# Attention and top-1 MoE: all shifts of a pair first on VectorE, one rotating PSUM pool of four banks, the selection steps at new slots

## The chip, the cores and the metric

The kernel runs on one core of one Trainium2 chip. The metric is the device time of one execution in microseconds. The engines are TensorE (PE; its weight loads are PEld), VectorE (DVE), ScalarE (ACT), GpSimd (POOL) and SyncE (SP), which issues most transfers. Each engine takes its instructions in the order in which they were written for it, and waits where one's input or buffer isn't ready.

## The reference

Causal attention over 8 batches of 12 heads (448 positions, 64 wide) feeds a mixture of 8 experts in which each token goes to one expert and each expert takes at most 80 tokens, those with the largest gate weight.

```python
scores = scale * np.matmul(q, k.transpose(0, 1, 3, 2))
scores = np.where(mask, -1000000000.0, scores)
scores = scores - np.max(scores, axis=-1, keepdims=True)
attn = np.exp(scores)
attn = attn / (np.sum(attn, axis=-1, keepdims=True) + 1e-09)
x = np.matmul(attn, v)                  # heads side by side: 3584 tokens x 768
logits = x @ w_gate                     # 8 experts
expert_idx = np.argmax(logits, axis=1)
gate_w = softmax(logits)[arange, expert_idx]
for e in range(8):
    tok_idx = the 80 tokens of expert e with the largest gate_w
    out[tok_idx] = gate_w[tok_idx, None] * (np.maximum(x[tok_idx] @ w1[e], 0) @ w2[e])
```

Tokens that no expert takes give rows of zeros.

## The kernel before

**The pairs.** Heads go two by two, 6 pairs to a batch, 48 in all. `pairs` is one list, and the loop over it takes three pairs at once in a software pipeline: at step i the scores of pair i are normalized, the probabilities of pair i-1 are transposed, and pair i-2 is multiplied with the values. A step has 8 slots (`SLOTS`), and the order of the code in a slot is the order on the engines. Two pairs are a third (`PH`): GpSimd splits the next third's q and k in two f16 parts (`split_third`, L370 and L402) while this one runs.

**One step.** TensorE first multiplies pair i-2's probabilities with v (`xp`, eight products), then the scores of the pair's first block (three `corner` products to `sp`). In slots 1, 2, 4 and 5 (`TSLOT`) it transposes four groups of four blocks of pair i-1 (`tp`). In the last slot it makes the 18 score products of pair i+1 (`sp`), in four banks.

VectorE "shifts" each of the seven score tiles of pair i: one instruction adds the mask, negates, and leaves the row's minimum in `nb` (L446, to `ns`). ScalarE raises it to a power with `nb` as its bias (L449, `prob`). Tiles come in the order (0,0), (0,1), (1,0), (1,1), (2,0), (2,1), first; they are 192, 192, 320, 320, 448, 448 and 64 wide, and slot k holds the shift and the power of tile k. ScalarE also copies each group of transposes to `PT` (L486) in slots 2 to 5; of the fourth group two small pieces are copied by VectorE. VectorE copies `xp` to `xu` (L509) in slot 2 (`XSLOT`).

**The selection.** After a batch's six pairs come its gate and its selection, in steps spread over the slots of the next pairs. `STEPS` names the slot, counted from the batch's end, and `later_on` files the step under it: `gp`/`gs` gate products and their copy, `lp`/`lg`/`logit` logits by token and their largest, `chosen` to `parts` the one-hot and the weight in three parts, `r0t` to `r1c` their transposes (`selt`) and copies (`ex`), `rl`/`lt`/`cp`/`ro` the comparison with the tokens kept so far, `c3w` to `c0l` the comparison of the batch's tokens with each other (`rn`, `less`), `gt`/`own`/`earlier`/`rank` the ranks, `places` (`rm`), `rr`, `tn`, `tab`, `rp` and `row` the new table of kept tokens. `ROWS0` and `ROWS1` place eight row groups: TensorE transposes `xu` back (`rt`), VectorE scales (`xr`), and SyncE writes the token rows (`xs`). `norms` inverts the sums (L533) and copies a part of them to `rql` on ScalarE.

**PSUM.** There are eight banks: four for scores (`ps_s`), two for transposes (`ps_t`), two for all the rest (`ps_m`: `xp` and every tile of the selection and the row groups, through `bank`). A request waits until the tile that had the bank last has been read.

**After the pairs.** `TAIL` is the written order of the last batch's rest, and after it come the experts: two layers each, with weights loaded by SyncE and split by ScalarE and VectorE.

Of the kernel before, what the change touches and what calls it, by code (L numbers as in the profile page):

```python
# [7 lines left out]
F32 = mybir.dt.float32  # L8
# [4 lines left out]
AF = mybir.ActivationFunctionType  # L13
ALU = mybir.AluOpType
# [3 lines left out]
P = 128  # L18
DH = 64
QB = 64  # L20
MASKED = -8.0e9
HUGE = 3.0e38
TSLOT = [1, 2, 4, 5]
CSLOT = [2, 3, 4, 5]
XSLOT = 2
NORMS = [0, 2, 2]
ROWGAP = 1
ROWS0 = [3, 6, 9, 11]
ROWS1 = [20, 22, 25, 45]
STEPS = {'gp': 13, 'gs': 14, 'lp': 18, 'lg': 18, 'logit': 19, 'shifted': 20, 'chosen': 21, 'sums': 22, 'one_hot': 23, 'weight': 23, 'columns': 24, 'weighted': 25, 'parts': 26, 'r0t': 29, 'r0c': 30, 'r1t': 31, 'r1c': 32, 'rl': 33, 'lt': 34, 'c3w': 35, 'c3l': 36, 'cp': 37, 'ro': 38, 'c2w': 38, 'c2l': 39, 'c1w': 40, 'c1l': 40, 'c0w': 41, 'c0l': 41, 'places': 42, 'gt': 44, 'own': 44, 'earlier': 44, 'rank': 45, 'rr': 47, 'tn': 50, 'tab': 50, 'rp': 53, 'row': 54}  # L30
THIRD = [0, 0, 2, 2, 4, 6, 8]
THIRD_EARLY = [0, 2, 4, 6, 6, 8, 9]
SECOND = [5, 6, 7, 8, 9, 10, 11]
# [13 lines left out]
def attention_then_moe(  # L47
# [30 lines left out]
    wearly = ctx.enter_context(tc.tile_pool(name="wearly", bufs=1))  # L78
    sel_stack = ExitStack()
    spool = sel_stack.enter_context(tc.tile_pool(name="sel", bufs=2, side="right"))  # L80
    ps_m = ctx.enter_context(tc.tile_pool(name="ps_m", bufs=2, space=PSUM))
    att = ExitStack()
    akeep = att.enter_context(tc.tile_pool(name="akeep", bufs=1))
    apool = att.enter_context(tc.tile_pool(name="att", bufs=2))
    turn_stack = ExitStack()
    ps_t = turn_stack.enter_context(tc.tile_pool(name="ps_t", bufs=2, space=PSUM))
    score_stack = ExitStack()
    ps_s = score_stack.enter_context(tc.tile_pool(name="ps_s", bufs=4, space=PSUM, side="right"))
    ps_x = None

    def bank(shape, dtype, name):
        return (ps_x or ps_m).tile(shape, dtype, name=name, tag="x" if ps_x else "misc")

    row_banks, row_pool = [], []

# [312 lines left out]
    def scores_groups(pr, n):  # L408

        st = state[pr.b * HB + pr.p // PH]  # L410
        p = pr.p % PH
        pr.P = prob[n % 2]
        pr.sp = {}

        def products():
            q_hi, q_lo, k_hi, k_lo = st["parts"]
            banks = [ps_s.tile([P, 512], F32, name="sp", tag="sp") for _ in range(4)]
            for j in range(2):
                pr.sp[0, j] = banks[j][:, 0:WIDTH[0]]
                pr.sp[1, j] = banks[j][:, WIDTH[0]:WIDTH[0] + WIDTH[1]]  # L420
                pr.sp[2, j] = banks[2 + j][:, 0:WIDTH[2]]
            pr.sp["first"] = banks[2][:, WIDTH[2]:WIDTH[2] + QB]
            for t in range(NT - 1):
                for x, (a, c) in enumerate(((q_hi, k_hi), (q_lo, k_hi), (q_hi, k_lo))):
                    for j, rows in enumerate((lo, hi)):
                        nc.tensor.matmul(pr.sp[t, j], a[rows, p, queries(t)], c[rows, p, FROM[t]:FROM[t] + WIDTH[t]], start=(x == 0),  # L426
                                         stop=(x == 2))
# [7 lines left out]
        def after(t, j):
            h = t * H + 2 * pr.p + j
            return lambda: softmax(pr.sp[t, j], WIDTH[t], mask[:, MASK_AT[t]:MASK_AT[t] + WIDTH[t]], OFF[t, j], pr.sums[:, h:h + 1])

        def after_first():
            h = (NT - 1) * H + pr.p  # L440
            softmax(pr.sp["first"], QB, mask_0, OFF["first"], pr.sums[:, h:h + 1])

        def softmax(sp, w, m, off, total):
            ns = apool.tile([P, S], F32, name="ns", tag="ns", bufs=4)
            nb = apool.tile([P, 1], F32, name="nb", tag="nb", bufs=5)
            pr.masked = nc.vector.tensor_tensor_reduce(  # L446
                out=ns[:, 0:w], in0=sp, in1=m, scale=-1.0 / 8.0, scalar=HUGE, op0=ALU.add, op1=ALU.min,
                accum_out=nb)
            nc.scalar.activation(pr.P[:, off:off + w], ns[:, 0:w], AF.Exp, bias=nb, scale=-1.0, accum_out=total)  # L449

        return products, products_first, [after(t, j) for t in range(NT - 1) for j in range(2)] + [after_first]

    def transpose_groups(pr, n):

        pr.PT = flipped[n % 2]

        full = lambda t, j, at: pr.P[:, OFF[t, j] + at * QB:OFF[t, j] + at * QB + P]
        blocks = [
            [full(t, j, t) for j in range(2) for t in (0, 1)],
            [full(t, j, 2 * t + 1) for j in range(2) for t in (1, 2)],  # L460
            [full(2, j, at) for j in range(2) for at in (3, 1)],
            [full(0, j, 2) for j in range(2)] + [full(2, j, -1) for j in range(2)],
        ]
        ways = [
            [(slice(0, P), 0, [[256, 2], [1, 256]], COL[0] + QB, [[WPT, 2], [1, 256]])],
            [(slice(0, P), 0, [[256, 2], [1, 256]], COL[1] + QB, [[WPT, 2], [1, 256]])],
            [(slice(0, P), 0, [[256, 2], [P, 2], [1, P]], COL[0] + S - P,
              [[WPT, 2], [COL[3] - P - (COL[0] + S - P), 2], [1, P]])],
            [(hi, QB, [[256, 2], [P, 2], [1, QB]], COL[2], [[COL[3] - COL[2], 2], [WPT, 2], [1, QB]]),
             (lo, QB, [[P, 2], [1, QB]], COL[1], [[WPT, 2], [1, QB]]),  # L470
             (lo, 256, [[QB, 2], [1, QB]], COL[0], [[WPT, 2], [1, QB]])],
        ]

        def group(g):
            got = []

            def work():
                tp = ps_t.tile([P, 4 * P], F32, name="tp", tag="tp")
                got.append(tp)
                for i, f in enumerate(blocks[g]):  # L480
                    nc.tensor.transpose(tp[:, i * P:(i + 1) * P], f, ident)  # L481

            def copy(x):
                rows, at, dims, to, todims = ways[g][x]
                way = nc.scalar.copy if x == 0 else nc.vector.tensor_copy
                way(part_of(pr.PT, rows, to, *todims), part_of(got[0], rows, at, *dims))  # L486
            return work, [lambda x=x: copy(x) for x in range(len(ways[g]))]
        return [group(g) for g in range(4)]

    def values_group(pr):  # L490
# [94 lines left out]
    def row_group(bt, t, g, how="v"):  # L585
# [5 lines left out]
        def turn():  # L591
            if ps_x:

                own = len(row_banks) % 2
                tp = (ps_t if own else ps_m).tile([P, NH, P], F32, name="rt", tag="tp" if own else "misc",
                                                  padded_shape=[P, 4, P])
# [98 lines left out]
    def select_groups(bt):  # L695
# [61 lines left out]
        def table_chunk(s):  # L757
# [15 lines left out]
                bt.lower.append((lower, sn))  # L773

            def counts():
                cp = got["cp"] = (ps_m.tile([SL, E], F32, name="cp", tag="misc") if last else bank([SL, E], F32, "cp"))
# [29 lines left out]
        def later_part(t):  # L806

            if t == NT - 1:
                bt.gt = ps_m.tile([P, NT, E], F32, name="gt", tag="misc")
# [133 lines left out]
    def batch_plan(bt):  # L943

        ends = (bt.b * NP + NP) * SLOTS
        for x, f in zip(NORMS, norms(bt, slice(0, NP))):
            later_on(ends + x, [f])
        for g, at in enumerate((ROWS0, ROWS1)):
            for t in range(NT):
                later_on(ends + at[t], row_group(bt, t, g), ROWGAP)  # L950

        steps = dict(zip(("gp", "gs"), gate_products(bt, range(NH))))
        steps.update(gate_steps(bt))
        if CAP:
            steps.update(select_groups(bt))
        for name, at in STEPS.items():
            if name in steps:
                later_on(ends + at, [steps.pop(name)])
        assert not steps
# [5 lines left out]
    with tc.manual_schedule():  # L965
# [26 lines left out]
        for i, pr in enumerate(pairs):  # L992
# [25 lines left out]
            for k in range(SLOTS):  # L1018
# [15 lines left out]
                if k == SLOTS - 1 and i + 1 < n:
# [386 lines left out]
```

## Time and profile before

| what | us |
|---|---|
| median of 3 runs | 598.86 (598.81 to 599.22) |
| the profiled execution | 603.67 |
| its span, from the first to the last instruction | 601.6 |
| busy in the span: PE, DVE, ACT, POOL | 472.4, 389.8, 405.0, 238.2 |
| first and last copy of xp to xu | 25.3 and 464.4 |

The profiled execution is 4.8 us above the median, and 2.07 us of it lie outside the span. The pairs end with the copy at 464.4; the rest of the last batch and the experts fill what is left of the span. In a row of the timeline the first number is the start in us from the span's start, the second the duration in us; what stands in brackets is how long the engine was idle before it, and what ended that. In a row of waits the numbers are the sum in us, the count and the longest. In a row of the chain of work that ended last, the two numbers are start and length.

### The profile page before, as it was taken

To read this page: it belongs to the slowest core of one execution; us is meant where nothing else is said; L and a number is where in the kernel's file an instruction comes from. 1 tells how busy PE (TensorE), PEld (TensorE's weight loads), DVE (VectorE), ACT (ScalarE), POOL (GpSimd) and SP (SyncE) were. 2 spreads that over 40 slices of the span, in tenths; PEclk is the share of its full clock that TensorE was granted. 3 is DMA by queue.
4 is the path that set the end of the run, shared out by engine and by line. 5 is a ranking of instruction groups with operands and counts; after the bars stand their busy time and mean duration, and the time that the engine had idled before them with its cause. 6 is when DMAs were issued, how large, how long until landed. Compare 5 with 4: busy or idle time off the path is not lost. (4 is left out here: it accounts for less than half of the span.)

```text
span 601.6 us, 15237 instructions
## 1 busy us (share of the span) xinstructions
PE 472.4 (79%) x5530; PEld 335.3 (56%) x5530; DVE 389.8 (65%) x1305; ACT 405.0 (67%) x1081; POOL 238.2 (40%) x345
## 2 busy tenths in 40 slices
PE   2878877887677777778777687788678899899995
PEld 1544454554354545545454454455445589899985
DVE  4554576556675565565655755656563789999993
ACT  3776766766666657565756665576654869998982
POOL 6636342526252543335243526142301442664321
PEclk9998999899999999897989998979897999999999
DMA  6333544456054515352525362343386379999971
GB/s 211 124 128 109 164 129 153 160 183 208 25 185 159 183 24 199 134 171 61 195 101 172 95 217 91 125 139 117 115 347 204 120 259 383 388 385 404 406 299 34
DMA packets 46666, 109.90 MB, mean 183 GB/s; under 512 B 5842, under 2 KB 23250, under 8 KB 45952
## 3 DMA queue, kind: packets, MB, share of 16 engines
q1 hardware_dynamic: 45392, 105.20, 50.0%
q0 software_dynamic: 1056, 3.51, 1.8%
q8 instruction: 43, 0.70, 0.5%
q14 instruction: 31, 0.25, 0.1%
q10 hardware_dynamic: 144, 0.23, 0.1%
HBM read 85.35 MB, written 23.99 MB: 182 GB/s over the span
## 5 line engine op out<-in xcount | busy, mean ns | idle before, releaser
L449 ACT ACTIVATE prob<-ns,nb 128x192 f32<-128x192 f32 (+3 forms) x336 | 177.4, 529 | 111.9 <-DVE nb L446 103.9
L481 PE MATMUL tp<-ident,prob 128*128 128x128 f32 x768 | 123.4, 291 | 59.9 <-ACT PT L486 59.6
L446 DVE CUSTOM_DVE_ANT_0 ns<-sp,mask 128x192 f32<-128x192 f32 (+3 forms) x336 | 138.2, 440 | 6.7 <-PE sp L426 3.8
L486 ACT COPY PT<-tp 128x512 f32<-128x512 f32 x192 | 100.2, 522 | 49.0 <-PE tp L481 47.3
L481 PEld LDWEIGHTS tp<-ident,prob 128*128 128x128 f32 x768 | 86.9, 146 | 81.0 <-ACT PT L486 77.5
L426 PE MATMUL sp<-qk 64*128 64x448 f16 (+2 forms) x864 | 85.8, 313 | 47.7 <-DVE nb L446 40.7
L504 PE MATMUL xp<-PT,vt 128*64 128x448 f32 (+3 forms) x768 | 104.7, 419 | 1.7 <-DVE PT L486 1.1
L370 POOL TENSOR_TENSOR qk<-qk,qk 128x448 f16<-128x448 f32 x93 | 97.1, 1061 | 14.5 <-DVE qk L402 8.7
L1150 DVE SCALAR_TENSOR_TENSOR wl<-wraw,wh 128x768 f16<-128x768 f32 (+1 forms) x98 | 97.3, 1059 | 1.9 <-POOL wl L1341 1.6
L504 PEld LDWEIGHTS xp<-PT,vt 128*64 128x64 f32 x768 | 55.2, 148 | 63.2 <-issue 30.6
L1165 ACT ACTIVATE wh<-wraw 128x768 f16<-128x768 f32 (+1 forms) x98 | 84.9, 927 | 3.8 <-ACT yt L1292 0.9
L426 PEld LDWEIGHTS <-qk 64*128 64x128 f16 x864 | 38.3, 98 | 84.3 <-issue 66.4
L486 DVE COPY PT<-tp 64x128 f32<-64x128 f32 x96 | 23.1, 278 | 91.6 <-ACT PT L486 91.6
L1226 PEld LDWEIGHTS <-wh 128*128 128x128 f16 x668 | 67.1, 100 | 3.8 <-issue 3.8
L1228 PEld LDWEIGHTS <-wh 128*128 128x128 f16 x668 | 66.7, 100 | 2.0 <-issue 1.9
L1229 PEld LDWEIGHTS <-wl 128*128 128x128 f16 x668 | 66.7, 100 | 0.9 <-issue 0.9
L509 DVE COPY xu<-xp 128x448 f32<-128x448 f32 x48 | 29.9, 624 | 55.8 <-PE xp L504 55.8
L449 ACT ACTIVATION_READ_ACCUMULATOR prob<-ns,nb 128x1 f32 x336 | 63.3, 188 | 0.0
L402 POOL CAST qk<-qk 128x896 f16<-128x896 f32 x40 | 36.5, 931 | 51.3 <-PE sp L426 43.5
L1307 POOL DMA_INDIRECT out<-yo,idx x8 | 34.7, 4341 | 54.8 <-ACT yo L1304 51.6
L1228 PE MATMUL op<-hl,wh 128*128 128x80 f16 x324 | 36.9, 202 | 1.3 <-issue 1.3
L1229 PE MATMUL op<-hh,wl 128*128 128x80 f16 x324 | 36.9, 202 | 1.2 <-issue 1.2
(175 smaller groups left out, 669.6 us busy)
## 6 DMA issues: line engine op xcount, KB each, us to landing
wraw<-w SPq DMA_DIRECT2D x48, 384.0 KB, 9.5
wraw<-w SPq DMA_DIRECT2D x30, 512.0 KB, 9.8
out<-mask SPq DMA_DIRECT2D x56, 192.0 KB, 2.5
qk<-k_t SPq DMA_DIRECT2D x23, 448.0 KB, 4.0
qk<-q_t SPq DMA_DIRECT2D x23, 448.0 KB, 4.1
vt<-v_t SPq DMA_DIRECT2D x24, 384.0 KB, 7.8
xs<-xr SPq DMA_DIRECT2D x42, 192.0 KB, 1.8
wraw<-w SPq DMA_DIRECT2D x5, 1536.0 KB, 7.8
```

The lines of the kernel that those rows point to most:

```text
L370: sub = lambda e, o, a, b: e.tensor_tensor(out=o, in0=a, in1=b, op=ALU.subtract)
L426: nc.tensor.matmul(pr.sp[t, j], a[rows, p, queries(t)], c[rows, p, FROM[t]:FROM[t] + WIDTH[t]], start=(x == 0), stop=(x == 2))
L446: pr.masked = nc.vector.tensor_tensor_reduce(out=ns[:, 0:w], in0=sp, in1=m, scale=-1.0 / 8.0, scalar=HUGE, op0=ALU.add, op1=ALU.min, accum ...
L449: nc.scalar.activation(pr.P[:, off:off + w], ns[:, 0:w], AF.Exp, bias=nb, scale=-1.0, accum_out=total)
L481: nc.tensor.transpose(tp[:, i * P:(i + 1) * P], f, ident)
L486: way(part_of(pr.PT, rows, to, *todims), part_of(got[0], rows, at, *dims))
L504: nc.tensor.matmul(xp[rows, c * P:S], st["vt"][:, c, p * P + j * DH:p * P + (j + 1) * DH], pr.PT[:, j, n0:n0 + w], start=(c == 0), stop=(c ...
L1150: return nc.vector.scalar_tensor_tensor(out=l, in0=src, scalar=SW, in1=h, op0=ALU.mult, op1=ALU.subtract)
L1165: nc.scalar.activation(h, src, AF.Copy, scale=SW)
L1226: nc.tensor.matmul(o, wh[:, ws], ah[:, c, :], start=(x == 0 and i % per == 0), stop=False, skip_group_check=True)
L1228: nc.tensor.matmul(o, wh[:, ws], al[:, c, :], start=False, stop=False, skip_group_check=True)
L1229: nc.tensor.matmul(o, wl[:, ws], ah[:, c, :], start=False, stop=(x == n - 1), skip_group_check=True)
```

## The change

1. **Shifts first.** `softmax` returns the shift and the power apart. `SHIFTED` puts the shifts of a pair in slots 0, 0, 1, 1, 2, 3, 3, with the copy of `xp` to `xu` ahead of the fifth. The powers stay in slots 0 to 6. `ns` has a tag for each width with two buffers (before: one tag, four buffers), `nb` has nine (before five).
2. **The VectorE pieces of the fourth transposes** move to slot 6 (`COPIED`), behind all seven shifts.
3. **PSUM.** `ps_m` and `ps_t` become one pool `ps_g` of four banks in rotation: `xp`, `tp`, and every tile of the selection and the row groups. The experts get a `ps_m` of their own later. The first block's scores (`first`) go to the fourth bank, no longer to the third.
4. **Slots.** A row group names its two slots apart. `STEPS` runs to slot 71 (before: 54), with most readers on VectorE in slots 4 to 7 of a step, behind the shifts. `EARLY` is the table for the last batch but one.

```diff
-CSLOT = [2, 3, 4, 5]
+COPIED = {2: (0, 0), 3: (1, 0), 4: (2, 0), 5: (3, 0), 6: (3, 1)}
+SHIFTED = [0, 0, 1, 1, 2, 3, 3]
-ROWGAP = 1
-ROWS0 = [3, 6, 9, 11]
-ROWS1 = [20, 22, 25, 45]
+ROWS0 = [(2, 4), (4, 5), (6, 7), (10, 12)]
+ROWS1 = [(26, 28), (28, 29), (34, 36), (42, 44)]
...
-    ps_m = ctx.enter_context(tc.tile_pool(name="ps_m", bufs=2, space=PSUM))
-    ps_t = turn_stack.enter_context(tc.tile_pool(name="ps_t", bufs=2, space=PSUM))
+    ps_g = turn_stack.enter_context(tc.tile_pool(name="ps_g", bufs=4, space=PSUM))
...
-            pr.sp["first"] = banks[2][:, WIDTH[2]:WIDTH[2] + QB]
+            pr.sp["first"] = banks[3][:, WIDTH[2]:WIDTH[2] + QB]
...
-        def softmax(sp, w, m, off, total):
-            ns = apool.tile([P, S], F32, name="ns", tag="ns", bufs=4)
-            nb = apool.tile([P, 1], F32, name="nb", tag="nb", bufs=5)
-            pr.masked = nc.vector.tensor_tensor_reduce(
-                out=ns[:, 0:w], in0=sp, in1=m, scale=-1.0 / 8.0, scalar=HUGE, op0=ALU.add, op1=ALU.min,
-                accum_out=nb)
-            nc.scalar.activation(pr.P[:, off:off + w], ns[:, 0:w], AF.Exp, bias=nb, scale=-1.0, accum_out=total)
+            def shift():
+                ns = apool.tile([P, w], F32, name="ns", tag=f"ns{t}", bufs=2)
+                nb = apool.tile([P, 1], F32, name="nb", tag="nb", bufs=9)
+                got.extend((ns, nb))
+                nc.vector.tensor_tensor_reduce(
+                    out=ns, in0=pr.sp[x], in1=m, scale=-1.0 / 8.0, scalar=HUGE, op0=ALU.add, op1=ALU.min, accum_out=nb)
+
+            def power():
+                nc.scalar.activation(pr.P[:, OFF[x]:OFF[x] + w], got[0], AF.Exp, bias=got[1], scale=-1.0,
+                                     accum_out=pr.sums[:, h:h + 1])
+            return shift, power
...
-                tp = ps_t.tile([P, 4 * P], F32, name="tp", tag="tp")
+                tp = ps_g.tile([P, 4 * P], F32, name="tp", tag="g")
...
-            return work, [lambda x=x: copy(x) for x in range(len(ways[g]))]
+            return work, [lambda: copy(0), lambda: [copy(x) for x in range(1, len(ways[g]))]]
...
-        for name, at in STEPS.items():
+        for name, at in (EARLY if bt.b == B - 2 else STEPS).items():
...
+                for x, at in enumerate(SHIFTED):
+                    if at == k:
+                        if values and k == XSLOT:
+                            values[1]()
+                        afters[x][0]()
                 if k < len(afters):
-                    afters[k]()
-                if turns and k in CSLOT:
-                    for f in turns[CSLOT.index(k)][1]:
-                        f()
-                if values and k == XSLOT:
-                    values[1]()
+                    afters[k][1]()
+                if turns and k in COPIED:
+                    g, x = COPIED[k]
+                    turns[g][1][x]()
...
+    ps_m = ctx.enter_context(tc.tile_pool(name="ps_m", bufs=2, space=PSUM, reuse_waits="tile"))
```

How the rows stand now. First VectorE, in the fifth pair after a batch's end, from the copy of `xp` on. The shifts are the rows of L446 (after: L445); each has a second row that leaves `nb`, which isn't shown. Before:

```order
L509 COPY xu<-xp 128x448
L771 TENSOR_SCALAR lt,lower_3612<-rl,ggw 128x80 x4
L446 ISA ns,nb<-sp,mask 128x320
L446 ISA ns,nb<-sp,mask 128x448
L752 SCALAR_TENSOR_TENSOR less_3461,parts<-rn,ggw,before 128x512
L446 ISA ns,nb<-sp,mask 128x448
L486 COPY PT_117<-tp 64x2x64 x2
L446 ISA ns,nb<-sp,mask_89 128x64
```

After:

```order
L511 COPY xu<-xp 128x448
L445 ISA ns,nb<-sp,mask 128x448
L445 ISA ns,nb<-sp,mask 128x448
L445 ISA ns,nb<-sp,mask_86 128x64
L621 TENSOR_TENSOR xr<-rt,sums 128x384
L771 TENSOR_SCALAR lt,lower_3633<-rl,ggw 128x80 x4
L752 SCALAR_TENSOR_TENSOR less_3403,parts<-rn,ggw,before 128x512
L488 COPY PT_114<-tp 64x2x64 x2
L752 SCALAR_TENSOR_TENSOR less_3402,parts<-rn,ggw,before 128x384
```

The comparisons stood between the shifts, and now stand between the last shift and the PT copies, where a row group's `xr` stands too; the second comparison follows the PT copies.

TensorE in the same pair, from the first transposes to the scores of the next pair (weight loads and equal rows left out). Before:

```order
L481 MATMUL tp<-ident,prob_111 128x128 x4
L765 MATMUL rl<-row_0_701,ex 128x80
L481 MATMUL tp<-ident,prob_111 128x128 x4
L749 MATMUL rn<-ex 128x512
L481 MATMUL tp<-ident,prob_111 128x128 x8
L778 MATMUL cp<-oh_693,lt 80x8
```

After:

```order
L483 MATMUL tp<-ident,prob_108 128x128 x4
L765 MATMUL rl<-row_0_707,ex 128x80
L483 MATMUL tp<-ident,prob_108 128x128 x4
L602 MATMUL rt<-ident,xu 128x128 x3
L483 MATMUL tp<-ident,prob_108 128x128 x4
L749 MATMUL rn<-ex 128x512
L483 MATMUL tp<-ident,prob_108 128x128 x4
L749 MATMUL rn<-ex 128x384
```

A row group now stands here, `cp` went to the next pair, and the products of 512 columns stand ahead of the fourth transposes; by the rotation their bank is that of `rl`, four requests earlier.

VectorE at the ranks, up to the next pair's first shift. Before, they stood in the sixth step after their batch's end:

```order
L823 TENSOR_TENSOR own<-gt,goh 128x32
L825 TENSOR_REDUCE larger<-own 128x4
L446 ISA ns,nb<-sp,mask 128x448
L486 COPY PT_116<-tp 64x2x64 x2
L446 ISA ns,nb<-sp,mask_89 128x64
L621 TENSOR_TENSOR xr<-rt,rql 64x384
L841 TENSOR_TENSOR rr<-rank,slots_t 128x320
L446 ISA ns,nb<-sp,mask 128x192
```

After, they stand in the seventh, which is the first after the next batch's end:

```order
L823 TENSOR_TENSOR own<-gt,goh 128x32
L825 TENSOR_REDUCE larger<-own 128x4
L621 TENSOR_TENSOR xr<-rt,sums 128x384 x2
L488 COPY PT_114<-tp 64x2x64 x2
L841 TENSOR_TENSOR rr<-rank,slots_t 128x320
L621 TENSOR_TENSOR xr<-rt,sums 128x384
L445 ISA ns,nb<-sp,mask 128x192
```

Two row groups now stand ahead of the PT copies, and `rr` with one row group behind them, ahead of the next pair's shifts.

More of the change, by code (lines that the diff above doesn't have):

```diff
@@ L23 @@
 TSLOT = [1, 2, 4, 5]
-CSLOT = [2, 3, 4, 5]
+COPIED = {2: (0, 0), 3: (1, 0), 4: (2, 0), 5: (3, 0), 6: (3, 1)}
+SHIFTED = [0, 0, 1, 1, 2, 3, 3]
 XSLOT = 2
 NORMS = [0, 2, 2]
-ROWGAP = 1
-ROWS0 = [3, 6, 9, 11]
-ROWS1 = [20, 22, 25, 45]
-STEPS = {'gp': 13, 'gs': 14, 'lp': 18, 'lg': 18, 'logit': 19, 'shifted': 20, 'chosen': 21, 'sums': 22, 'one_hot': 23, 'weight': 23, 'columns': 24, 'weighted': 25, 'parts': 26, 'r0t': 29, 'r0c': 30, 'r1t': 31, 'r1c': 32, 'rl': 33, 'lt': 34, 'c3w': 35, 'c3l': 36, 'cp': 37, 'ro': 38, 'c2w': 38, 'c2l': 39, 'c1w': 40, 'c1l': 40, 'c0w': 41, 'c0l': 41, 'places': 42, 'gt': 44, 'own': 44, 'earlier': 44, 'rank': 45, 'rr': 47, 'tn': 50, 'tab': 50, 'rp': 53, 'row': 54}
+ROWS0 = [(2, 4), (4, 5), (6, 7), (10, 12)]
+ROWS1 = [(26, 28), (28, 29), (34, 36), (42, 44)]
+STEPS = {'gp': 12, 'gs': 13, 'lp': 16, 'lg': 20, 'logit': 20, 'shifted': 21, 'chosen': 22, 'sums': 23, 'one_hot': 23, 'weight': 23, 'columns': 23, 'weighted': 24, 'parts': 24, 'r0t': 29, 'r0c': 30, 'r1t': 30, 'r1c': 31, 'rl': 33, 'lt': 36, 'c3w': 36, 'c3l': 37, 'c2w': 38, 'c2l': 39, 'cp': 41, 'ro': 44, 'c1w': 42, 'c1l': 44, 'c0w': 44, 'c0l': 45, 'gt': 49, 'own': 52, 'earlier': 46, 'rank': 53, 'rr': 55, 'places': 60, 'tn': 66, 'tab': 68, 'rp': 70, 'row': 71}
+EARLY = {'gp': 12, 'gs': 13, 'lp': 16, 'lg': 20, 'logit': 20, 'shifted': 21, 'chosen': 22, 'sums': 23, 'one_hot': 23, 'weight': 23, 'columns': 23, 'weighted': 24, 'parts': 24, 'r0t': 29, 'r0c': 30, 'r1t': 30, 'r1c': 31, 'rl': 33, 'lt': 36, 'c3w': 34, 'c3l': 36, 'c2w': 36, 'c2l': 37, 'c1w': 38, 'c1l': 38, 'cp': 39, 'ro': 40, 'c0w': 39, 'c0l': 40, 'gt': 42, 'own': 44, 'earlier': 41, 'rank': 44, 'places': 45, 'rr': 46, 'tn': 49, 'tab': 49, 'rp': 52, 'row': 53}
 THIRD = [0, 0, 2, 2, 4, 6, 8]
@@ L91, in bank @@
     def bank(shape, dtype, name):
-        return (ps_x or ps_m).tile(shape, dtype, name=name, tag="x" if ps_x else "misc")
+        return (ps_x or ps_g).tile(shape, dtype, name=name, tag="x" if ps_x else "g")
     row_banks, row_pool = [], []
@@ L433, in products_first, with softmax @@
                 nc.tensor.matmul(pr.sp["first"], d[:, a, p, :], c[:, p, FROM[0]:FROM[0] + QB], start=(x == 0), stop=(x == 2))
[L435 to L441, printed above, removed]
-        def softmax(sp, w, m, off, total):
-            ns = apool.tile([P, S], F32, name="ns", tag="ns", bufs=4)
-            nb = apool.tile([P, 1], F32, name="nb", tag="nb", bufs=5)
-            pr.masked = nc.vector.tensor_tensor_reduce(
-                out=ns[:, 0:w], in0=sp, in1=m, scale=-1.0 / 8.0, scalar=HUGE, op0=ALU.add, op1=ALU.min,
-                accum_out=nb)
-            nc.scalar.activation(pr.P[:, off:off + w], ns[:, 0:w], AF.Exp, bias=nb, scale=-1.0, accum_out=total)
-        return products, products_first, [after(t, j) for t in range(NT - 1) for j in range(2)] + [after_first]
+        def softmax(x):
+            t, j = (NT - 1, 0) if x == "first" else x
+            w, m = (QB, mask_0) if x == "first" else (WIDTH[t], mask[:, MASK_AT[t]:MASK_AT[t] + WIDTH[t]])
+            h = t * H + (pr.p if x == "first" else 2 * pr.p + j)
+            got = []
+            def shift():
[8 more added lines that the diff above has]
+            return shift, power
+        return products, products_first, [softmax((t, j)) for t in range(NT - 1) for j in range(2)] + [softmax("first")]
     def transpose_groups(pr, n):
@@ L592, in turn @@
             if ps_x:
-                own = len(row_banks) % 2
-                tp = (ps_t if own else ps_m).tile([P, NH, P], F32, name="rt", tag="tp" if own else "misc",
-                                                  padded_shape=[P, 4, P])
+                tp = ps_g.tile([P, NH, P], F32, name="rt", tag="g", padded_shape=[P, 4, P])
                 row_banks.append(tp)
@@ L775, in counts @@
             def counts():
-                cp = got["cp"] = (ps_m.tile([SL, E], F32, name="cp", tag="misc") if last else bank([SL, E], F32, "cp"))
+                cp = got["cp"] = (ps_g.tile([SL, E], F32, name="cp", tag="g") if last else bank([SL, E], F32, "cp"))
                 for t in range(NT):
@@ L808, in later_part @@
             if t == NT - 1:
-                bt.gt = ps_m.tile([P, NT, E], F32, name="gt", tag="misc")
+                bt.gt = ps_g.tile([P, NT, E], F32, name="gt", tag="g")
             for u in range(t + 1):
@@ L947, in batch_plan @@
             later_on(ends + x, [f])
-        for g, at in enumerate((ROWS0, ROWS1)):
+        for g, rows in enumerate((ROWS0, ROWS1)):
             for t in range(NT):
-                later_on(ends + at[t], row_group(bt, t, g), ROWGAP)
+                for at, f in zip(rows[t], row_group(bt, t, g)):
+                    later_on(ends + at, [f])
         steps = dict(zip(("gp", "gs"), gate_products(bt, range(NH))))
```

## The prediction

> **What bounds the kernel now.** I read the page's busy shares first, then the waits of the stretch in which only attention pairs run (60 to 440 us), then one pair in order of time.
>
> ```profile
> span 601.6 us, 15237 instructions
> PE 472.4 (79%) x5530; PEld 335.3 (56%) x5530; DVE 389.8 (65%) x1305; ACT 405.0 (67%) x1081; POOL 238.2 (40%) x345
> ...
> ACT prob L449 <- DVE nb L446: 87.2, 118, 2.4
> DVE PT L486 <- ACT PT L486: 74.0, 40, 2.3
> ...
> DVE xu L509 <- PE xp L504: 41.8, 30, 2.3
> PE sp L426 <- DVE nb L446: 33.7, 30, 2.0
> ```
>
> No engine is full, and each waits for the others: ScalarE for VectorE's shifts, VectorE for ScalarE's copies and for TensorE's xp, TensorE for VectorE's shifts. That is a ring, one turn per pair, so the time is the number of pairs times the length of a turn. The length is read between two copies of xp to xu. Here is a pair early in the program, with almost no selection work in it.
>
> ```profile
> 40.94 1.07 PE L481 MATMUL tp<-ident,prob 128*128 128x128 f32 x8
> 40.96 0.63 DVE L509 COPY xu<-xp 128x448 f32<-128x448 f32 x1 [1.20 <-PE xp L504]
> 41.67 0.58 ACT L486 COPY PT<-tp 128x512 f32<-128x512 f32 x1 [1.16 <-PE tp L481]
> ...
> 42.44 0.62 DVE L446 CUSTOM_DVE_ANT_0 ns<-sp,mask 128x448 f32<-128x448 f32 x1
> 42.99 0.62 DVE L446 CUSTOM_DVE_ANT_0 ns<-sp,mask 128x448 f32<-128x448 f32 x1
> 43.92 1.01 PE L426 MATMUL sp<-qk 64*128 64x192 f16 x13
> 45.09 0.37 ACT L486 COPY PT<-tp 64x256 f32<-64x256 f32 x1
> 45.49 0.48 DVE L486 COPY PT<-tp 64x128 f32<-64x128 f32 x2 [1.88 <-ACT PT L486]
> 45.90 0.21 DVE L446 CUSTOM_DVE_ANT_0 ns<-sp,mask 128x64 f32<-128x64 f32 x1
> 46.04 0.34 DVE L446 CUSTOM_DVE_ANT_0 ns<-sp,mask 128x192 f32<-128x192 f32 x1
> 46.17 0.72 PE L426 MATMUL sp<-qk 64*128 64x448 f16 x5 [1.23 <-DVE nb L446]
> 46.56 0.44 ACT L449 ACTIVATE prob<-ns,nb 128x192 f32<-128x192 f32 x1
> 46.82 1.95 PE L504 MATMUL xp<-PT,vt 128*64 128x448 f32 x16
> 48.82 0.62 DVE L509 COPY xu<-xp 128x448 f32<-128x448 f32 x1 [1.74 <-PE xp L504]
> ```
>
> The turn is 48.82 - 40.96 = 7.86 us, and its legs follow each other without a gap: 0.71 to ScalarE's first copy of transposes (41.67), 3.79 until the fourth copy ends (45.09 + 0.37 = 45.46), 0.44 for VectorE's two PT copies (to 45.90), 0.27 for the seventh shift (until TensorE goes on at 46.17), 0.65 for the last five score products (to 46.82), 2.00 for xp and its way to xu. The seventh shift stands in this ring only because VectorE takes it behind the PT copies.
>
> ```profile
> L509 DVE COPY xu<-xp x48: 615/624/627, 25.3 to 464.4; 128x448 f32<-128x448 f32 x48
> 458.87 0.62 DVE L509 COPY xu<-xp 128x448 f32<-128x448 f32 x1 [2.91 <-PE xp L504]
> ```
>
> Over 46 turns, from 25.3 to 458.87, the mean is 433.6 / 46 = 9.43 us. So 1.57 us a turn come on top of the plain 7.86: selection work, row groups and slow TensorE stretches.
>
> **The plain turn after the change.** All shifts now stand ahead of the PT copies, so the legs of 0.27 and 0.65 leave: the seventh shift is done and all 18 score products can run before the fourth copy. What follows the PT copies is xp itself. This hop isn't seen in the pair above; the nearest rows are at the end of attention.
>
> ```profile
> 461.76 0.49 DVE PT L486 x2
> 462.38 1.95 PE xp L504 x16
> ```
>
> The PT copies end at 462.25 and xp starts at 462.38: 0.13 us. The turn becomes 7.86 - 0.92 + 0.13 = 7.07 us.
>
> Each cover, counted from xu's start. VectorE: xu 0.54 (40.96 to the next start is about that), two shifts of 0.55 (42.44 to 42.99), the short one 0.14 (45.90 to 46.04): done at 1.8. TensorE: four groups of transposes, at most 1.07 / 2 each, 2.14, and the scores 1.01 + 0.72: done at 3.9, while xp is due at 0.71 + 3.79 + 0.44 + 0.13 = 5.07. If either went over 5.07, the excess would be paid. VectorE's front behind the PT copies: two shifts of 0.34 and two that are shorter than the 0.55 of the widest, at most 1.8 in all, while xu is due 0.13 + 2.00 after them: it isn't late. ScalarE: the first power starts about 0.4 after the PT copies, and 0.44 + 0.44 + 0.56 (the row of 344.10 below) end 1.8 after them, while the first copy is due at 0.13 + 2.00 + 0.71 = 2.8: one microsecond is spare. The larger ns and nb buffers cost no instruction. First's move from bank 2 to bank 3 frees bank 2 a shift earlier, and costs nothing since that lies under the same cover.
>
> **The selection and row work.** VectorE has 4.5 - 1.8 = 2.7 us a turn in which it waits for the fourth copy, and most of the selection now stands there. A wait of VectorE there (for rt, lp, rn, gt, tn) holds no shift and no power. What remains on the ring I take turn by turn, six to a batch, counted from a batch's end.
>
> ```profile
> 280.35 0.47 DVE L841 TENSOR_TENSOR rr<-rank,slots_t 128x320 bf16<-128x320 f16 x1
> 338.81 0.55 DVE L621 TENSOR_TENSOR xr<-rt,rql 64x384 f32<-64x384 f32 x1
> 339.28 1.35 DVE L841 TENSOR_TENSOR rr<-rank,slots_t 128x320 bf16<-128x320 f16 x1
> 343.23 0.40 DVE L533 RECIPROCAL sums<-sums 128x42 f32<-128x42 f32 x1
> 344.10 0.56 ACT L449 ACTIVATE prob<-ns,nb 128x320 f32<-128x320 f32 x1
> 354.51 1.70 PE L554 MATMUL gp<-xu,wgd 128*32 128x448 f32 x12
> ...
> 356.22 1.33 PE sp L426 x18
> 360.53 0.35 PE lp L568 x4
> 360.90 0.61 DVE lg L580 x2
> 380.74 0.97 DVE lt L771 x8
> ```
>
> - First turn: the reciprocal stands behind xu and one shift, at 1.09. From its start to the power behind the rql copies is 344.10 - 343.23 = 0.87, so that power starts at 1.96 in place of 0.71 + 0.58 = 1.29: 0.67.
> - From it to the second turn: rr (0.47 to 1.35) and one xr (0.47, 338.81 to just before 339.28) stand behind the PT copies, and push all four front shifts back by 0.9 to 1.8. One microsecond is spare: between 0 and 0.8, I take 0.4.
> - Second turn: gp, 1.65 us of TensorE ahead of the fourth transposes; 2.14 + 1.65 + 1.33 = 5.1 before xp, with one row group beside it (rt): 0.2.
> - Third turn: lp (0.35) stands ahead of the first transposes. It also holds a bank until lg has read it, behind xu, the shifts and tab at about 2.6, and the third transposes want that bank: 0.3 more, 0.65.
> - Fourth turn: two row groups and selt end before 5.07: 0.
> - Fifth turn: rn for 512 columns wants the bank that lt reads. Lt is through at 1.8 + 0.47 (xr) + 0.97 = 3.2; then come rn, the fourth transposes (0.53), rn again and the scores (1.33): about 5.6 in place of 5.07, so 0.5.
> - Sixth turn: the third transposes want cp's bank, which ro frees behind an xr, at 2.4: 0.25.
>
> Together 2.67 a batch, 0.45 a turn. The bounds are 0 and the present 1.57. I take the worked value, since nearly every piece has a row. GpSimd is moved past too: rank now stands between two of its splits. It is busy 40% of the span, and the split that waits for rank has more than one turn left until scores read it: nothing. SP's queue issues the same transfers in nearly the same order: nothing, and if a load came late, a third's first scores would wait.
>
> **The sum.** 46 x (7.07 + 0.45) = 345.9 us in place of 433.6: 87.7 less. Two things go back. TensorE's slow passes:
>
> ```profile
> 55.15 3.12 PE L504 MATMUL xp<-PT,vt 128*64 128x448 f32 x16
> 426.51 3.47 PE L504 MATMUL xp<-PT,vt 128*64 128x448 f32 x16
> PEclk9998999899999999897989998979897999999999
> ```
>
> These are the first and the last of eight passes of xp that took 2.3 us or more in place of 1.95, in slices where the granted clock is below 9 tenths or just at it. My legs have the fast clock. With fewer stalls I expect four to remain at about 1.4 each, 5.6. And 0.1 a turn for hops that no row shows, of the size of the 0.13 above, 4.6. That leaves 77.5. The expert layers behind attention aren't touched, beyond a pool that is opened later: 0. The profiled execution took 603.67 (span 601.6 and 2.07 around it); less 77.5 it is 526.2. It stood 4.8 above the median of 598.86, so I forecast **521 us**. This case's own range is 502 to 536: no slow passes, no hops and extras of 0.27 a turn at the one end (10.2 + 46 x 0.18 = 18 lower), extras of 0.75 at the other (46 x 0.30 = 14 higher, and a little).
>
> [...] The clock is the term that could turn. In the plain pair above, only transposes ran between the xp before 40.94 and the scores at 43.92, 3 us, and the next xp still took 1.95, the fast value. [...]
>
> **Rivals.**
> - *Banks of the one pool are held longer than I worked out.* A selection tile now blocks the transposes behind it, where before it blocked only its own kind. If the extras are 1.0 a turn, 46 x 0.55 = 25 is lost: 546 (536 to 565). For: every one of these tiles is read behind the shifts. Against: 2.7 us of room.
> - *Only the ring shortens, the extras stay.* 46 x 0.79 = 36 is gained, and 598.86 becomes 563. Against: the wait of ScalarE for VectorE, 87.2 us, comes mostly from selection between the shifts, and that place is empty now.
> - *Half clock in each turn.* A slow xp costs 1.17 to 1.52 more by the two rows; 46 x 1.35 = 62, less the 5.6 in the sum, is 56: 577. Against: at present eight passes of 46 with more idle TensorE.
> - *Slower.* If the second group of transposes in each turn waits for a bank until VectorE is through with its selection, at 1.8 and another 1.6, the second copy starts at 3.4 + 0.53 + 0.1 = 4.0 in place of 0.71 + 0.58 + 0.56 = 1.85. The turn is 2.2 longer, and 521 + 46 x 2.2 = 622. It decides from (598.86 - 521) / 46 = 1.7 of such a hold in every turn. Against: by the order of requests, the second group's bank is that of four requests earlier, mostly a group whose copy is long done.
>
> **Chances.** My forecast 0.60, held banks 0.23, extras stay 0.06, half clock 0.05, slower 0.03, no difference 0.03 (within 0.2%, about what runs of this kernel can tell). Faster is 0.94. From 502 to 552 lie the forecast's range and two thirds of the held banks, near 0.8 with the tails left out.
>
> **What would show it.** In the trace after: xu to xu of 7.0 to 7.2 in the early pairs; the waits "ACT prob for DVE nb" and "PE sp for DVE nb" nearly gone; "DVE PT for ACT PT" still there, but shorter by the selection moved in front of it; xp waiting for the PT copies. The forecast is wrong if transposes wait for VectorE's readers (a bank held), if xu is late behind the front shifts, or if slow passes of xp are more than eight.

## The result: 507.9 us, and the profile after

The changed kernel takes 507.93 us (median of 507.27 to 508.78), before 599.04: a ratio of 0.848, interval 0.846 to 0.850. The time came out 13 us under the forecast of 521, inside its range.

From the page after: the span, the busy times, and the clock that TensorE was granted in 40 slices.

```profile
span 505.7 us, 15362 instructions
...
PE 435.1 (86%) x5530; PEld 330.8 (65%) x5530; DVE 384.5 (76%) x1305; ACT 399.5 (79%) x1081; POOL 240.8 (48%) x345
...
PEclk9999999999999999999999999999999999999999
```

DVE and ACT work as long as before (384.5 and 389.8, 399.5 and 405.0): little was saved in work, nearly all in waiting. PE's busy time fell by 37 us. No slice has a low clock any more, but that is only a part of it: 11 us are the 48 passes of xp (104.7 to 93.6), which had slow ones among them. The score products account for 16 (85.8 to 70.1): they now run in one row of 18 (1.40 us in the pair below), where the pair shown before had 13 and 5 (1.01 and 0.72). The transposes account for 12 (123.4 to 111.5).

The waits of the attention pairs after, longest first (sum in us, count, longest):

```profile
DVE PT L488 <- ACT PT L488: 57.9, 42, 2.2
...
ACT prob L449 <- DVE nb L445: 33.3, 34, 1.4
ACT PT L488 <- PE tp L483: 21.3, 29, 2.2
...
DVE xu L511 <- PE xp L506: 16.2, 23, 1.8
```

ScalarE's wait for VectorE fell from 87.2 to 33.3, VectorE's wait for xp from 41.8 to 16.2, and TensorE's wait for the shifts, 33.7 before, is no longer in the list. The forecast had ScalarE's wait nearly gone. Of what is left, 32.5 us stand ahead of the first power of a pair, behind the front shifts, where the forecast had counted one microsecond as spare. VectorE still waits for the fourth copy: that wait is in the ring.

A plain turn after, between two copies of xp to xu, as the timeline has it:

```profile
38.88 0.62 DVE L511 COPY xu<-xp 128x448 f32<-128x448 f32 x1 [0.18 <-PE xp L506]
...
39.60 0.59 ACT L488 COPY PT<-tp 128x512 f32<-128x512 f32 x1 [0.91 <-PE tp L483]
...
40.51 0.22 DVE L445 CUSTOM_DVE_ANT_0 ns<-sp,mask 128x64 f32<-128x64 f32 x1
...
40.75 1.40 PE L426 MATMUL sp<-qk 64*128 64x192 f16 x18
...
43.03 0.37 ACT L488 COPY PT<-tp 64x256 f32<-64x256 f32 x1
...
43.43 0.48 DVE L488 COPY PT<-tp 64x128 f32<-64x128 f32 x2 [2.16 <-ACT PT L488]
...
44.06 1.95 PE L506 MATMUL xp<-PT,vt 128*64 128x448 f32 x16 [1.91 <-DVE PT L488]
...
46.05 0.62 DVE L511 COPY xu<-xp 128x448 f32<-128x448 f32 x1 [0.76 <-PE xp L506]
```

The seventh shift is done at 40.73 and the 18 score products at 42.15, both under the cover of ScalarE's copies and powers. The fourth copy ends at 43.40, VectorE's PT copies follow, and xp starts behind them. The turn is 7.17 us here and 7.11 to 7.12 in the three other plain turns at the start, where the forecast had 7.07 and the kernel before 7.86.

### The profile page after: what moved, and what is told of

Same layout as the page of the kernel before. It is cut to its first block, busy times and chain, and to the rows that moved or that the text cites. A ratio compares the mean times of both kernels' runs of the same rounds, so it can differ in the third digit from the quotient of the medians.

```text
span 505.7 us, 15362 instructions
## 1 busy us (share of the span) xinstructions
PE 435.1 (86%) x5530; PEld 330.8 (65%) x5530; DVE 384.5 (76%) x1305; ACT 399.5 (79%) x1081; POOL 240.8 (48%) x345
## 4 chain that ended last, share of the span: by engine, by line
PE 59%; ACT 19%; issue 10%; DVE 8%; DMA 1%; POOLq 0%; ACTq 0%; POOL 0%; DVEq 0%
PE xp L506 18%; ACT prob L449 12%; PE tp L483 8%; ACT PT L488 7%; PE sp L426 5%; DVE ns L445 3%; PE hp L1224 3%; PE gp L556 3%; PE hp L1233 3%; PE hp L1231 3%; PE hp L1234 2%; PE op L1231 2%; PE op L1233 2%; PE op L1234 2%; PE rt L602 2%
## 5 line engine op out<-in xcount | busy, mean ns | idle before, releaser
L445 DVE CUSTOM_DVE_ANT_0 ns<-sp,mask 128x192 f32<-128x192 f32 (+3 forms) x336 | 131.8, 440 | 4.4 <-PE sp L433 3.1
L506 PE MATMUL xp<-PT,vt 128*64 128x448 f32 (+3 forms) x768 | 93.6, 385 | 30.7 <-ACT prob L449 11.7
L483 PE MATMUL tp<-ident,prob 128*128 128x128 f32 x768 | 111.5, 280 | 9.5 <-ACT PT L488 9.0
L506 PEld LDWEIGHTS xp<-PT,vt 128*64 128x64 f32 x768 | 57.1, 136 | 80.4 <-ACT prob L449 30.4
L370 POOL TENSOR_TENSOR qk<-qk,qk 128x448 f16<-128x448 f32 x93 | 98.5, 1074 | 13.2 <-PE xp L506 8.6
L483 PEld LDWEIGHTS tp<-ident,prob 128*128 128x128 f32 x768 | 84.3, 142 | 25.0 <-ACT PT L488 14.9
L426 PE MATMUL sp<-qk 64*128 64x448 f16 (+2 forms) x864 | 70.1, 304 | 7.1 <-DVE qk L381 5.4
L426 PEld LDWEIGHTS <-qk 64*128 64x128 f16 x864 | 36.9, 95 | 29.2 <-issue 10.9
L402 POOL CAST qk<-qk 128x896 f16<-128x896 f32 x40 | 38.8, 988 | 13.3 <-PE sp L433 8.9
L1231 PE MATMUL op<-hh,wh 128*128 128x80 f16 x324 | 37.0, 202 | 1.6 <-issue 1.6
```

The lines of the kernel that those rows point to most:

```text
L370: sub = lambda e, o, a, b: e.tensor_tensor(out=o, in0=a, in1=b, op=ALU.subtract)
L445: nc.vector.tensor_tensor_reduce(out=ns, in0=pr.sp[x], in1=m, scale=-1.0 / 8.0, scalar=HUGE, op0=ALU.add, op1=ALU.min, accum_out=nb)
L506: nc.tensor.matmul(xp[rows, c * P:S], st["vt"][:, c, p * P + j * DH:p * P + (j + 1) * DH], pr.PT[:, j, n0:n0 + w], start=(c == 0), stop=(c ...
L1231: nc.tensor.matmul(o, wh[:, ws], ah[:, c, :], start=(x == 0 and i % per == 0), stop=False, skip_group_check=True)
```

## The experiments

Each kernel computes the whole reference. Ratios are to the kernel before, run beside it.

**Is it the ring? (b_seventh)** The kernel before, with VectorE's PT pieces behind the seventh shift and nothing else:

```diff
-                    for f in turns[CSLOT.index(k)][1]:
-                        f()
+                    turns[CSLOT.index(k)][1][0]()
+                if turns and k == 6:
+                    for f in turns[3][1][1:]:
+                        f()
```

> The kernel before, with one edit: VectorE's two PT pieces stand behind the seventh shift, which itself keeps its slot among the others' waits. Theory: the ring loses 0.27 + 0.65 and gains the hop of 0.13, 46 x 0.79 = 36, and the slow TensorE passes that follow the wait for that shift become fewer (up to 11): 553 to 566 us. Rival, with selection still among the shifts another wait takes the place: 585 us or more.

565.03 us, ratio 0.941 (0.935 to 0.947), at the upper end of the range. One of its four executions took 570.70, at a clock of 0.965. Its plain turns are 7.12 to 7.17 us, like those of the changed kernel. Moving two small copies behind one short shift is worth some 35 us of the 91 (599, or 601.6 run beside it, to 565). Not all of that is the ring. In the profiled executions 46 turns are 36.6 us shorter, and 10 of these are slow passes of xp, one in place of nine. The other 26 are 0.58 a turn in place of the 0.79 worked out; the second turn of a batch, for one, isn't shorter at all (8.70 before, 8.72 here).

**And the other way round (a_seventh)** The changed kernel with only the seventh shift behind the PT copies again:

```diff
-SHIFTED = [0, 0, 1, 1, 2, 3, 3]
+SHIFTED = [0, 0, 1, 1, 2, 3, 7]
...
+                if k == 7:
+                    afters[6][1]()
```

> The changed kernel with the seventh shift and its power back behind the PT copies. Theory: the last five or more score products wait for that shift again, so 0.27 + 0.65 us come back into the ring and the hop of 0.13 leaves: 46 x 0.79 = 36 more, about 544 us (538 to 560), and a plain turn of 7.9 us. Rival, the place of one narrow shift is not what bounds: within 3 us of 508.

553.95 us, 0.922 (0.918 to 0.926): 46 more than the changed kernel, 10 more than the 36 that the ring's leg was put at. Its plain turns are 7.81 to 7.86, as expected, and the six turns of a batch without slow passes are longer by 0.77 in the mean, 35 us in 46 turns. Most of the rest is TensorE's clock. Here its timeline shows TensorE waiting for that shift, and the pass of xp behind the wait at 3.62 us in place of 1.95:

```profile
128.44 1.01 PE L426 MATMUL sp<-qk 64*128 64x192 f16 x13
131.25 0.72 PE L426 MATMUL sp<-qk 64*128 64x448 f16 x5 [1.79 <-DVE nb L445]
131.91 3.62 PE L506 MATMUL xp<-PT,vt 128*64 128x448 f32 x16
```

Six turns are stretched by slow passes in this way, and a seventh pass, at 407.25, takes 2.50. The mean granted clock is 0.975, against 0.962 before and 0.999 after.

**Shifts first, alone (a_shifts), with the old pools (a_pools), with the old slots (a_steps)** The pools of two and two banks and the old tables, put back singly and together. The move of the first block's scores to the fourth bank stays in all of them; it wasn't put back on its own:

```diff
-    ps_g = turn_stack.enter_context(tc.tile_pool(name="ps_g", bufs=4, space=PSUM))
+    ps_m = ctx.enter_context(tc.tile_pool(name="ps_m", bufs=2, space=PSUM))
+    ps_t = turn_stack.enter_context(tc.tile_pool(name="ps_t", bufs=2, space=PSUM))
...
-ROWS0 = [(2, 4), (4, 5), (6, 7), (10, 12)]
+ROWS0 = [(3, 4), (6, 7), (9, 10), (11, 12)]
```

> The changed kernel with both the old PSUM pools and the old slots: the shifts first with their own buffers, alone. Theory: the shifts' order gives the shorter ring (7.86 to 7.1, 36 us) and takes some selection off it; about 535 us (525 to 550). Rival, the parts only work together: 560 us or more. Rival, this part is all of it: 506 to 515 us.

529.28 us, 0.882 (0.879 to 0.885). Its 46 turns are 73.7 us shorter than before. If the plain turn's gain (7.86 to 7.12) is had in each, it makes 34 of them, and the slow passes of xp, of which none is left, make 11. The other 29 I put down to selection work that stood between the shifts; no run takes that apart.

> The changed kernel with the two old PSUM pools (two banks for transposes, two for all the rest) in place of the one of four. Ring theory (the time is the ring copy of xp, first transposes, ScalarE's copies and powers, PT copies, xp): with two transpose banks the third group waits for the first copy (1.2 us after xu) and the fourth for the second (2.2 us), both before the fourth copy is due at 4.1, so the ring is not longer: 508 to 516 us. Rival, the single pool is what lets TensorE run ahead and is a main part of the gain: 530 us or more, with transposes waiting for ScalarE's copies in the groups that end the turn.

514.41 us, 0.857 (0.854 to 0.861).

> The changed kernel with the old slots of the selection steps and of the row groups. Theory: the ring of a plain turn stays 7.1 us, but selection readers stand again between the shifts and ahead of the PT copies in slots 0 to 3, so the extras of 0.3 us a turn go up to about 0.8: 46 x 0.5 = 23 more, about 531 us (520 to 545). Rival, the selection is hidden wherever it stands once the shifts are first: 506 to 512 us. Rival on the other side, the spread is most of the gain: 555 us or more.

520.95 us, 0.867 (0.864 to 0.870): at the low end of what I had expected. The extras went from 0.26 to 0.58 a turn, not to 0.8.

So all shifts first make about 70 of the 91 us (599.0 to 529.3). The new slots are worth 15 beside the old pools (529.3 to 514.4) and 13 beside the new one (521.0 to 507.9), the new pool 8 beside the old slots (529.3 to 521.0) and 6.5 beside the new ones (514.4 to 507.9). The three nearly add up. In a_pools every turn is at most 0.33 longer, except one, of 11.42 us in place of 7.99, in which the selection of the last batch but one runs, which is packed more tightly:

```profile
357.48 0.47 DVE L755 SCALAR_TENSOR_TENSOR less<-rn,ggw,before 128x256 bf16<-128x256 f32 x1
358.00 0.22 PE L752 MATMUL rn<-ex 128*128 128x128 bf16 x1 [1.13 <-DVE less L755]
358.15 1.40 PE L427 MATMUL sp<-qk 64*128 64x192 f16 x18
...
359.94 3.57 PE L507 MATMUL xp<-PT,vt 128*64 128x448 f32 x16 [0.39 <-DVE ro L786]
```

The last comparison's product (rn) waits for a bank that VectorE reads only behind its PT copies; the next pair's scores stand behind it on TensorE, and the pass of xp after that is slow. This one turn is about half of what the new pool is worth beside the new slots.

**The own buffers (a_bufs)** One tag of four for ns and five for nb, as before:

```diff
-                ns = apool.tile([P, w], F32, name="ns", tag=f"ns{t}", bufs=2)
-                nb = apool.tile([P, 1], F32, name="nb", tag="nb", bufs=9)
+                ns = apool.tile([P, S], F32, name="ns", tag="ns", bufs=4)
+                nb = apool.tile([P, 1], F32, name="nb", tag="nb", bufs=5)
```

> The changed kernel with the old buffers: one tag of four for ns, five for nb. Theory: the fifth shift wants the buffer of the first, whose power is done before the first copy of transposes, and each later one likewise finds a power that is done, so the own buffers are worth nothing: 506 to 511 us. Rival, they are what lets the shifts run first: 520 us or more, with shifts waiting for ScalarE.

508.21 us, 0.843 (0.840 to 0.847): no difference, though its profiled execution has one slow pass of xp (3.63 us). The added buffers are worth nothing here.

**Does TensorE's wait make its clock slow? (a_warm)** In a_seventh, work for TensorE in that wait, from the tenth pair on:

```diff
+                if t == 2 and n > 8:
+                    wm = ps_g.tile([P, S], F32, name="wm", tag="g")
+                    for _ in range(5):
+                        nc.tensor.matmul(wm, identb, before[:, 0:S], start=True, stop=True)
```

> The kernel of a_seventh with five products of 448 columns on constants, which nothing reads, put on TensorE ahead of the score products of the widest block, where it waits for the seventh shift (about 1 us of work in a wait of 1.8). Theory: the slow passes of xp (six in a_seventh's trace, each behind such a wait) come from TensorE standing idle, so with that wait filled they go, and the time falls by about 1.4 for each though work is added: 544 to 549 us, granted clock 0.99. Rival, the slow passes come at their own times whatever TensorE does: 554 us or more, clock 0.975.

554.71 us, 0.922 (0.918 to 0.926), clock 0.989. The clock half came as the theory has it: the four executions have 0.984 to 0.991, those of a_seventh 0.975 to 0.980. Behind 80 us, where the filler is, a_seventh's trace has four turns stretched by slow passes, and this one none of them; only the pass at 407 is slow in both. The time half didn't come. The filler itself lengthens the second turn of a batch (7.81 to 8.45, six times), the fifth (7.86 to 8.25, five times) and two turns of the last batch (by 0.52 and 0.25), 6.6 us together, which is what the four slow passes cost (6.5). It shows that work put into that wait takes these slow passes away, and that filling it with idle work isn't free.

The two page lines, first a_seventh, then a_warm:

```profile
PEclk9999899998999899999989999998989999999998
```

```profile
PEclk9998999999999999999999999999989999999999
```

**The ring, one leg further (v_one, v_two)** If the ring bounds, the two wide powers that stand between ScalarE's copies are paid in each turn though nobody waits for them until the next. `POWERS` puts a slot's powers ahead of its copies (0) or behind them (1).

```diff
+POWERS = {(0, 0): [0], (1, 0): [1], (2, 0): [2], (3, 0): [3], (5, 1): [4, 5], (6, 0): [6]}
-COPIED = {2: (0, 0), 3: (1, 0), 4: (2, 0), 5: (3, 0), 6: (3, 1)}
+COPIED = {2: [(0, 0), (1, 0)], 5: [(2, 0), (3, 0), (3, 1)]}
```

This is v_two. In v_one the copies keep their slots, and powers 4 and 5 stand behind the third and the fourth copy.

> The changed kernel with ScalarE's order altered: the wide power between the second and the third copy of transposes goes behind the third copy, and that between the third and the fourth behind the fourth. Theory: a power leaves the ring wherever it can go behind the fourth copy; here one of the two wide ones does (0.66), the other only changes places, so a turn of 7.1 becomes 6.45 where TensorE's own work allows it: about 484 us (475 to 493). Rival, TensorE (86% busy) is the bound now: 500 us or more.

493.70 us, 0.819 (0.816 to 0.823). The plain turn is 6.47, as expected; the time is 0.7 above the range, since the third, the sixth and the first turn of a batch take 7.45, 7.37 and 8.15 (7.55, 7.36 and 7.93 in the changed kernel).

> The changed kernel with all four copies of transposes ahead of the three last powers on ScalarE, and VectorE's PT pieces right behind them. Theory: both wide powers (1.33 us) leave the ring; a turn would be 5.75, but TensorE's own work of a turn is 5.2 and 6.2 with selection and row groups, so TensorE bounds at about 6.6: 472 us (460 to 485). Rival, TensorE is the bound now: 500 us or more. Rival on the other side, VectorE's selection ahead of the PT pieces is late: 490 to 500 us.

480.04 us, 0.797 (0.793 to 0.800): 28 us faster than the changed kernel, within the range, 8 over its middle. The plain turn of v_two in its timeline:

```profile
34.96 0.62 DVE L512 COPY xu<-xp 128x448 f32<-128x448 f32 x1 [0.18 <-PE xp L507]
...
35.68 1.08 ACT L489 COPY PT<-tp 128x512 f32<-128x512 f32 x2
...
36.63 0.57 ACT L450 ACTIVATE prob<-ns,nb 128x320 f32<-128x320 f32 x1
...
37.19 0.98 ACT L489 COPY PT<-tp 128x512 f32<-128x512 f32 x2
...
38.19 0.67 ACT L450 ACTIVATE prob<-ns,nb 128x448 f32<-128x448 f32 x1
38.20 0.48 DVE L489 COPY PT<-tp 64x128 f32<-64x128 f32 x2 [0.85 <-ACT PT L489]
...
38.83 1.95 PE L507 MATMUL xp<-PT,vt 128*64 128x448 f32 x16 [0.60 <-DVE PT L489]
...
40.81 0.62 DVE L512 COPY xu<-xp 128x448 f32<-128x448 f32 x1 [0.76 <-PE xp L507]
```

The power of 38.19 now runs beside the PT copies and xp. The turn is 5.85 here and 5.80 and 5.81 beside it, where 5.75 was worked out. The selection turns are 6.2 to 7.7, one in the last batch is 8.46, and TensorE is 91% busy.

**A last leg (v_three, v_four)** In v_two the first turn of a batch is 7.26, and ScalarE's rql copies stand in it ahead of the third copy.

```diff
-NORMS = [0, 2, 2]
+NORMS = [0, 2, 3]
```

> The kernel of v_two with ScalarE's two rql copies one slot later, behind the fourth power. Theory: they no longer stand ahead of the third copy, so the first turn of a batch falls from 7.26 to about 6.9, seven times: 477 to 478 us. Rival, TensorE's own work bounds that turn: 480 us as before.

480.20 us, 0.798 (0.795 to 0.800): no difference. The edit didn't do what the expectation says: slot 3 is still ahead of the third copy, only behind the fourth power. With slot 5 in place of 3:

> The kernel of v_two with the rql copies in slot 5, now really behind all four copies of transposes and the two widest powers (in v_three they still stood ahead of the third copy, behind one power: 7.15 us for the first turn in place of 7.26). Theory: ScalarE's 0.40 leaves the ring of that turn, but its three row groups, rr and the score products keep TensorE busy for about 6.6, so 6.7 to 7.0 us and 477 to 479 us in all. Rival, TensorE already bounds the turn: 7.1 and 480 us.

478.36 us, 0.794 (0.790 to 0.798), the fastest of all; its first turns are 6.79 to 6.85, as expected. Against v_two the difference in time is within the intervals; in the turns of the trace it is plain. One turn in the last batch took 10.05 in place of 8.46. Its score products took 2.58 us in place of the 1.40 of the same place in v_two, and its pass of xp 2.35 in place of 1.95: a slow stretch of TensorE.

```profile
324.92 2.58 PE L427 MATMUL sp<-qk 64*128 64x192 f16 x18
...
327.43 2.35 PE L507 MATMUL xp<-PT,vt 128*64 128x448 f32 x16
```

## Why the prediction was right, step by step

The mechanism was right: the ring, the two legs that leave it, and the cover under which the seventh shift and the scores run. The kernel before with that one leg changed (565) and the changed kernel with it put back (554) bracket it, and v_one and v_two shorten the same ring by the legs worked out for them. In both bracketing runs some 10 us are TensorE's slow passes and not the leg.

The sum was 13 us too high, and the terms say where. From the first copy of xp to the 47th, 46 turns, it had 345.9 + 5.6 + 4.6 = 356.1; the trace has 363.66 - 24.66 = 339.0:

```profile
24.66 0.62 DVE L511 COPY xu<-xp 128x448 f32<-128x448 f32 x1 [0.17 <-PE xp L506]
...
363.66 0.62 DVE L511 COPY xu<-xp 128x448 f32<-128x448 f32 x1 [1.69 <-PE xp L506]
```

- *The plain turn:* 7.07 and 0.1 for unseen hops; measured 7.11 (the first turn). 2.8 us too much.
- *Slow passes:* four were left in the sum, 5.6 us; there are none. The clock of this execution is 0.999. The forecast had counted eight before; there are nine, the last of them in the 46th turn (shown below).
- *The extras:* 0.45 a turn forecast, 0.26 measured (339.0 / 46 - 7.11): 8.7 us too much. By turn, in the batch from 141.68 us on, less 7.11: 0.83, 0.16, 0.44, -0.06, -0.01, 0.25, where the forecast had 0.67 + 0.4, 0.2, 0.65, 0, 0.5, 0.25.
- *Outside the turns* 166.7 us of span, 168.0 before: nearly untouched, as forecast.
- *The step from the profiled execution to the median* was -4.8, taken over from before. After, the profiled execution (507.38) stands 0.55 below the median. That adds 5.4 the other way, and hides nearly a third of the other errors, by luck.

```profile
455.15 3.68 PE L504 MATMUL xp<-PT,vt 128*64 128x448 f32 x16 [0.61 <-DVE nb L446]
```

The step that failed is the one on banks: that a request gets the bank of four requests earlier, as the description of the change has it too. The fifth turn's 0.5 and half of the third's 0.65 rest on it. In the third turn lp itself was paid as forecast (ScalarE's first copy comes 0.32 later than in the plain turn), but the third and fourth transposes didn't wait for lg, which reads lp until 159.47:

```profile
158.57 1.09 PE L483 MATMUL tp<-ident,prob 128*128 128x128 f32 x8
...
159.23 0.24 DVE L582 TENSOR_TENSOR lg<-lp,rql 64x96 f32<-64x96 f32 x1
```

The timeline of the fifth turn:

```profile
173.25 0.57 ACT L488 COPY PT<-tp 128x512 f32<-128x512 f32 x1
...
173.73 0.29 DVE L771 TENSOR_SCALAR_CACHE_REDUCE lt<-rl,ggw 128x80 bf16<-128x80 f32 x1
173.88 0.38 PE L749 MATMUL rn<-ex 128*128 128x512 bf16 x1 [0.37 <-ACT PT L488]
...
174.39 0.30 DVE L771 TENSOR_SCALAR_CACHE_REDUCE lt<-rl,ggw 128x80 bf16<-128x80 f32 x1
```

The product starts when ScalarE's second copy ends (173.82), while VectorE goes on reading rl until 174.69. So it has the second transposes' bank, not rl's, and the wait is 0.37 us, off the ring. In the sixth turn the forecast of 0.25 was met for another reason than the one given:

```profile
180.34 0.57 ACT L488 COPY PT<-tp 128x512 f32<-128x512 f32 x1
...
180.83 0.21 DVE L783 TENSOR_SCALAR ro<-cp,pnum 80x8 f16<-80x8 f32 x1
...
180.96 0.66 PE L483 MATMUL tp<-ident,prob 128*128 128x128 f32 x4 [0.71 <-ACT PT L488]
```

The third transposes start at 180.96 behind ScalarE's copy (180.91), while ro, which reads cp, ends at 181.04. How the pool picks a bank I didn't measure: the rows fit one that gives out the bank whose reader stands earliest in the program, but only these three places were looked at.

The first turn's 0.83 is nearly all the reciprocal: the power behind the rql copies starts 1.95 us after xu (143.63), where the first power behind ScalarE's first copy starts 1.20 after it in the plain turn (40.08). That is 0.75 for a forecast of 0.67. The 0.4 for rr and its xr came to next to nothing. Rr took 0.47 here, the low end of its bounds, and with the one xr behind it the next shifts start 0.86 late; xu still follows the start of xp after 2.02 us, 1.99 in the plain turn.

```profile
147.38 0.47 DVE L841 TENSOR_TENSOR rr<-rank,slots_t 128x320 bf16<-128x320 f16 x1
...
147.77 0.54 DVE L621 TENSOR_TENSOR xr<-rt,sums 128x384 f32<-128x384 f32 x1
...
148.24 0.34 DVE L445 CUSTOM_DVE_ANT_0 ns<-sp,mask 128x192 f32<-128x192 f32 x1
```

Of the rivals, held banks were a real danger: with two banks for the selection, one turn went to 11.42. "Only the ring shortens" gave 563 as its time, and b_seventh, which is that case, took 565; that it comes so near is partly luck, since 26 us there are the ring and 10 the slow passes. The reason given against that rival, that ScalarE's 87.2 us come mostly from selection between the shifts, holds for half of them: 43 us stood ahead of the second to sixth power of a pair, 20 ahead of the first, and 24 ahead of the seventh, which is the ring itself. Half clock in each turn didn't come: in each plain turn TensorE runs two microseconds of transposes and 1.4 of score products and then waits 1.9 us ahead of xp, and not one pass of xp is slow. The Trainium skill's page "TensorE: Matmul & The Clock Gate", section "HAM oscillation", gives the rule that TensorE should have no idle gaps over about 3.4 us, and its Part 4 says that transposes don't count as busy in the same way. The four slow passes of a_seventh that go in a_warm don't come out of that rule: in the 12 us ahead of each, the longest stretch without products, transposes not counted, is 1.79 us.

## What to carry to other kernels

Where no engine is full and each waits for the others, write down the ring, leg by leg from one turn of the timeline, and ask of each leg whether anyone needs it in this turn; an instruction that merely stands in a queue between two legs is paid in full, with what waits for it (a short shift and the five score products behind it cost 0.8 us a turn, two powers that nobody waited for 1.3). Put back one part at a time: here the order made 70 of 91 us, the slots and the pool the rest, and the buffers nothing.

## What the hardware showed that I had not expected

TensorE's slow passes aren't told by the length of its waits alone. Waits of 1.9 us in each plain turn of the changed kernel left the clock at 0.999, while a wait of 1.79 in a_seventh stood ahead of a pass of xp that took 3.62 us in place of 1.95. What goes with them is the mean length of the turn for the same work. All kernels here with turns of 6.8 to 7.8 us have clocks of 0.990 to 0.999 in all their executions. A_seventh, with 8.35, has 0.975 to 0.980; b_seventh, with 8.63, has 0.965 to 0.986; the kernel before, with 9.43, has 0.956 to 0.970. Filling a wait of a_seventh raised it to 0.984 to 0.991 at the same length of turn. The slow passes themselves are at most 0.24 us of these means. That is an order and not a threshold: the ranges overlap, and single slow passes occur in the fast kernels too (one each in the profiled executions of a_bufs, a_pools and a_steps). The condition stays open.
